# First norm, block turns and tail of a fused hash-bucket attention and gated MLP on one core

## The chip, the cores and the metric

The kernel runs on one core of a Trainium2 chip. Its time is device microseconds (us) of one execution, and the figure for a kernel is the median of its runs. The kernel before has three runs: 349.73, 350.91 and 350.99 us, median 350.91. One more execution was recorded by the profiler; it took 349.72 us.

## The reference

Four batches, eight heads, 768 tokens, head dimension 64. Every query and key gets a bucket: six sign bits of its product with a 64x6 matrix. Attention is masked to pairs with equal buckets. Its output, with the heads side by side, is the input of a normed and gated two-layer network.

```python
q_bits = (np.einsum('bhsd,dk->bhsk', q, proj) > 0)      # 6 bits; k_bits alike
mask = q_bucket[:, :, :, None] == k_bucket[:, :, None, :]
scores = np.where(mask, scale * np.matmul(q, k.transpose(0, 1, 3, 2)), -1e9)
attn = softmax(scores); x = (attn @ v) as 3072 x 512
xn = x / np.sqrt(np.mean(x * x, axis=-1, keepdims=True) + 1e-06) * rms_g
g = xn @ w_gate; silu = g * (1.0 / (1.0 + np.exp(-g)))
out = (silu * (xn @ w_val)) @ w_out                     # 512 -> 1536 -> 512
```

## The kernel before

**Units.** The work is cut into 8 units u, one for each half of the 768 queries of a batch b = u // 2. A unit has 8 heads, handled as 4 pairs hp. A slot is one third of a head of a unit: 256 keys by 384 queries. So a unit has 24 slots (NS, L545) and the main loop 192 (L750 to L755). The first two units share the order (0,0), (0,1), (1,0), (1,1), then the other heads of unit 0, then those of unit 1; from slot 48 on, unit u has slots 24u to 24u+23, which this document calls stage u-1: stage 1 is slots 48 to 71, stage 2 is 72 to 95, and so on.

**Order.** It is written out by hand. Slot t issues the scores of slot t+1 (two matmuls, L336), the exp of its own (ScalarE, L348), and then everything that the list plan[t] holds, in the order in which it was put there with at(w, s, f), which means slot 24w+s (L551). Each engine takes its instructions in that order, and waits where an input or a buffer isn't ready. The product with the values (av, L361, in two parts), the sum of the constant part of the softmax (otmp, L376), the division (rcp L381 and x L383), the squares (sq, L388) and their sums (ssp, L392) follow the scores of a head by a few slots.

**Mask.** The scores' matmul carries extra rows with the sign bits (values of +-0.5 scaled), so that pairs with equal buckets stand out by a large number in the exponent. The bits come from: a turn of q and k (64 numbers of a token onto the partitions), a matmul with the 6 columns (d_ps), signs (L209) and, for pairs that need both heads in one tile, select (L215) on VectorE, and a small DMA each to the rows of the tile QK. The turned q and k are cast to fp16 into the same tile by GpSimd (cast_part L165 for pairs of batch 0 and the first two of batch 1, cast_pool L193 for the others). The first six pairs are turned by TensorE (turn_pe, L149); all others by VectorE in blocks of 32x32 (turn_dve L180, four instructions for a pair, in slots t to t+3), from loads made in blocks (load_blocks, 8 DMAs for a pair on SyncE's queue, and one for v). hash_one (L265) makes the bits of one pair, hash_two (L282) of two. v_prep (L304) casts the values to fp16, v_sum (L309 on) adds them by thirds, and v_mean (m_ps, cvb L323) makes the constant term of the softmax for a batch. A table, spots (L638), says in which slot each pair of batches 1 to 3 is loaded and turned.

**Network.** norm(u) (L399 to L412) adds the four partial sums of squares (ss, VectorE), makes mean plus epsilon (ms, GpSimd L405) and the power -0.5 (rstd, GpSimd L409), and scales the three row blocks of x (xn, VectorE L412). turn_x (L414) turns xn on TensorE (x_ps, L419) and scales it with rms_g (xnT, VectorE). Then come 12 times gate (g_ps) and value (v_ps, both L436) with tanh on ScalarE (L444) and two products on VectorE (a L453, ht L454), and in the next unit's slots the projections (y_ps, L465, 3 x 12 matmuls) and the stores. spread (L670) deals these pieces out over the 24 slots of a stage by cost, and puts a hash in front of the first whole piece at or behind its slot. The norm of unit 0 stands at slot 36 with its turns at 38, its gates start at slot 40; the norm of unit u stands at slot 24(u+1)+4. After the last slot there is a tail: projections 0 and 1 of unit 6, norm(7), its turns with the projections of block 2 between them, the gates and the projections of unit 7.

**Buffers.** PSUM has three banks that turn_pe, hashes, m_ps, x_ps, g_ps, v_ps and y_ps share in turn (bank, L80), two for scores of two banks each (s_ps), and one for o_ps. Eight load tiles, six QK tiles.

Of the kernel before, what the change touches and what calls it, by code (L numbers as in the profile page):

```python
# [8 lines left out]
FP32 = mybir.dt.float32  # L9
FP16 = mybir.dt.float16  # L10
AF = mybir.ActivationFunctionType
ALU = mybir.AluOpType
AX = mybir.AxisListType
# [5 lines left out]
DMODEL = H * D  # L19
DFF = 1536  # L20
NF = DFF // 128
# [10 lines left out]
def kernel(  # L32
# [12 lines left out]
    nc = tc.nc  # L45
    PSUM = bass.MemoryType.PSUM

    const = ctx.enter_context(tc.tile_pool(name="const", bufs=1))
# [4 lines left out]
    xpool = ctx.enter_context(tc.tile_pool(name="xpool", bufs=2))  # L53
    npool = ctx.enter_context(tc.tile_pool(name="npool", bufs=1))
    hpool = ctx.enter_context(tc.tile_pool(name="hpool", bufs=1))
    spool = ctx.enter_context(tc.tile_pool(name="spool", bufs=2))
# [9 lines left out]
    zeros16 = const.tile([128, 512], FP16, name="zeros16")  # L66
# [2 lines left out]
    own = const.tile([128, 1], FP32, name="own")  # L69
    ebias = const.tile([128, 1], FP32, name="ebias")  # L70
    mhalf = const.tile([128, 3], FP32, name="mhalf")
    gcol = const.tile([128, 4], FP32, name="gcol")
    wg = const.tile([128, 4, DFF], FP16, name="wg")
    wv = const.tile([128, 4, DFF], FP16, name="wv")
# [5 lines left out]
    def bank(name, shape=None, dt=FP32):  # L80
        return gps.tile(shape or [128, 512], dt, name=name, tag="g")
# [242 lines left out]


    sps, psb, ot = {}, {}, {}
    x, ssp, xn, xnT = {}, {}, {}, {}

    def scores(u, i):
        b, half = divmod(u, 2)  # L330
# [38 lines left out]
    def attn_out(u, hp):  # L369
        b = u // 2  # L370
        if hp == 0:
            x[u] = xpool.tile([128, 3, DMODEL], FP32, name="x")
            ssp[u] = xpool.tile([128, 4, 3], FP32, name="ssp")
        o = ot.pop((u, hp))
        tmp = spool.tile([128, 3, 2, 66], FP32, name="otmp")
        nc.vector.tensor_add(  # L376
            tmp[:, :, :, 0:65], o[:, :, :, 0:65],
            cvb[b % 2][:, 2 * hp : 2 * hp + 2, 0:65].unsqueeze(1).to_broadcast([128, 3, 2, 65]),
        )
        r = spool.tile([128, 3, 2, 1], FP32, name="rcp")  # L380
        nc.vector.reciprocal(r, tmp[:, :, :, 64:65])  # L381
        xd = x[u][:, :, 128 * hp : 128 * hp + 128]
        nc.gpsimd.tensor_mul(  # L383
            xd.rearrange("p c (h d) -> p c h d", h=2), tmp[:, :, :, 0:64],
            r.to_broadcast([128, 3, 2, 64]),
        )
        sq = spool.tile([128, 3, 128], FP32, name="sq")
        nc.gpsimd.tensor_mul(sq, xd, xd)  # L388
        return sq

    def sumsq(u, hp, sq):
        nc.vector.tensor_reduce(  # L392
            out=ssp[u][:, hp, :], in_=sq, op=ALU.add, axis=AX.X
        )


    ht, gts = {}, {}

    def norm(u):  # L399
        ss = spool.tile([128, 3], FP32, name="ss")  # L400
        nc.vector.tensor_reduce(
            out=ss, in_=ssp[u].rearrange("p h c -> p c h"), op=ALU.add, axis=AX.X
        )
        ms = spool.tile([128, 3], FP32, name="ms")
        nc.gpsimd.tensor_scalar(  # L405
            out=ms, in0=ss, scalar1=1.0 / DMODEL, scalar2=1e-6, op0=ALU.mult, op1=ALU.add
        )
        rstd = spool.tile([128, 3], FP32, name="rstd")
        nc.gpsimd.tensor_tensor(out=rstd, in0=ms, in1=mhalf, op=ALU.pow)  # L409
        xn[u] = npool.tile([128, 3, DMODEL], FP16, name="xn")  # L410
        for c in range(3):
            nc.vector.tensor_scalar_mul(xn[u][:, c, :], x[u][:, c, :], rstd[:, c : c + 1])  # L412

    def turn_x(u, c, act=False):  # L414
        if c == 0:
            xnT[u] = npool.tile([128, 4, HALF], FP16, name="xnT", bufs=2)
        ps = bank("x_ps", [128, 4, 128], FP16)
        for kt in range(4):
            nc.tensor.transpose(ps[:, kt, :], xn[u][:, c, kt * 128 : (kt + 1) * 128], ident16)  # L419
        dst = xnT[u][:, :, c * 128 : (c + 1) * 128]  # L420
        if act:
            for kt in range(4):
                nc.scalar.mul(dst[:, kt], ps[:, kt], gcol[:, kt : kt + 1])
        else:
            nc.vector.tensor_mul(dst, ps, gcol.unsqueeze(2).to_broadcast([128, 4, 128]))
# [34 lines left out]
    def project(u, c, f0, f1):  # L460
        if f0 == 0:
            obank[u, c] = bank("y_ps")
        y = obank[u, c]
        for ft in range(f0, f1):
            nc.tensor.matmul(  # L465
                y, ht[u][:, ft, c * 128 : (c + 1) * 128], wo[:, ft, :],
                start=(ft == 0), stop=(ft == NF - 1),
            )
# [6 lines left out]
    def store(u, c):  # L475
        ysb = spool.tile([128, DMODEL], FP32, name="ysb", bufs=3)
        nc.scalar.copy(ysb, obank.pop((u, c)))  # L477
        nc.sync.dma_start(out=rows_of(u, c), in_=ysb)
# [40 lines left out]
        nc.gpsimd.memset(own[32 * t : 32 * t + 6, :], 4.0 * BIT * BIT)  # L519
    nc.vector.memset(ebias, EBIAS)  # L520
    nc.vector.memset(mhalf, -0.5)
    nc.vector.memset(ones16, 1.0)
    nc.vector.tensor_copy(ident16, ident)
    for i in range(2):
# [2 lines left out]

    wz = ops.tile([128, 512], FP32, name="z_ps", tag="o")

    def idle(n):  # L530

        for _ in range(n):
            nc.tensor.matmul(wz, zeros16[:, 0:128], zeros16, start=True, stop=True)  # L533

    idle(8)

    def load_w(dst, src, kt, n):
# [7 lines left out]
    NS = 24  # L545
# [5 lines left out]
    def at(w, s, f, *a):  # L551
        plan[NS * w + s].append(lambda: f(*a))
# [4 lines left out]
    cast_part(0, 0, "k", 1, 0, 1)  # L557
    turn_pe(0, 0, 1, "k")
    idle(3)
    sign, move, _ = hash_direct(0, 0, (0,))  # L560
    turn_pe(0, 0, 1, "q", nc.scalar.copy)
    idle(2)
    for which, e in (("k", 0), ("k", 1), ("q", 0)):
        cast_part(0, 0, which, e, 1, 1)
# [56 lines left out]
        at(0, 39 + 3 * i, load_w, wo, moe_w_out, 6 * i, 6)  # L621


    for hp, ts in ((0, (8, 22, 23, 24, 25, 24, 26, 26, 28, 38)), (1, (12, 27, 28, 29, 30, 29, 37, 31, 33, 39))):
        tl, ts = ts[0], ts[1:]
        for w in "kq":
            at(0, tl, load_natural, nc.sync, 1, hp, w)
        at(0, tl, load_v, nc.sync, 1, hp)
        at(0, ts[0], new_pair, 1, hp)
        for t, hh, w in zip(ts[0:4], (0, 1, 0, 1), "kkqq"):  # L630
            at(0, t, turn_pe, 1, hp, hh, w)
        at(0, ts[4], cast_pool, 1, hp, "k")
        at(0, ts[5], cast_pool, 1, hp, "q")
        at(0, ts[6], hash_pair, 1, hp)
        at(0, ts[7], send_pair, 1, hp)
        at(0, ts[8], v_prep, 1, hp)
        at(2, 6 + 6 * hp, v_mean, 1, hp, 2, range(6))
    spots = {  # L638
        1: ((None, None, 20, 40), (None, None, 44, 52)),
        2: ((51, 57, 66, 72), (63, 67, 81, 87)),  # L640
        3: ((96, 100, 110, 114), (105, 111, 129, 135)),
    }
    sqs = {}

    def o_step(u, hp):
        sqs[u, hp] = attn_out(u, hp)

    def s_step(u, hp):
        sumsq(u, hp, sqs.pop((u, hp)))

    at(0, 36, norm, 0)
    for c in range(3):
        at(0, 38, turn_x, 0, c)
    for n, (u, h) in enumerate(order):
# [7 lines left out]


    SCORES, AV, PROJ, FEED, TURN = 330, 290, 216, 324, 220
    hashes = {t: (700, hash_one, 1, hp) for hp, t in ((2, 49), (3, 57))}
    for b, ts in ((2, (71, 93)), (3, (117, 141))):
        for i, t in enumerate(ts):
            hashes[t] = (1430, hash_two, b, 2 * i)

# [24 lines left out]
    for u in range(7):  # L694
# [11 lines left out]
        for i in range(9):  # L706
            c, n = divmod(i, 3)
# [12 lines left out]
    for b, (loads, turns) in spots.items():  # L720
        for hp in range(4):
            if (b, hp) in ONPE:
                continue
            t = loads[hp]
            at(0, t, load_blocks, nc.sync, b, hp)
            at(0, t, load_v, nc.sync, b, hp)
            t = turns[hp]
            at(0, t, new_pair, b, hp)
            at(0, t, turn_dve, b, hp, "k", 0)
            at(0, t + 1, turn_dve, b, hp, "k", 1)  # L730
            at(0, t + 2, cast_pool, b, hp, "k")
            at(0, t + 2, turn_dve, b, hp, "q", 0)
            at(0, t + 3, turn_dve, b, hp, "q", 1)
            at(0, t + 4, cast_pool, b, hp, "q")
            at(0, t + 5, v_prep, b, hp)
            if b > 1:
                at(0, t + 5, v_sum, b, hp)
                if hp % 2:
                    at(2 * b, 1 + hp, v_mean, b, hp - 1, 4)
            else:  # L740
                at(2 * b, 6 + 6 * hp, v_mean, b, hp, 2, range(6))
# [17 lines left out]
    for c in range(2):  # L759
        project(6, c, 0, NF)  # L760
        store(6, c)
    norm(7)
    for c in range(3):
        turn_x(7, c, c == 1)
        project(6, 2, 4 * c, 4 * c + 4)
    store(6, 2)
    for ft in range(NF):
        for f in (gate, value):
# [36 lines left out]
```

## Time and profile before

| | before |
|---|---|
| median of the runs | 350.91 us (349.73 to 350.99) |
| profiled execution | 349.72 us |
| its span, first to last instruction | 347.9 us |
| mean granted TensorE clock | 0.99 |
| TensorE matmul (PE) | 331.9 us busy, 95% |
| VectorE (DVE) | 242.4 us, 70% |
| ScalarE (ACT) | 225.5 us, 65% |
| GpSimd (POOL) | 149.0 us, 43% |
| read from HBM, written | 28.32 MB, 6.29 MB |
| scores / gates and values | 94.4 / 165.6 us of PE |
| av / projections | 56.8 / 68.0 us of PE, in the group's rows (these overlap a little) |

How to read the profile. Busy times are sums over an engine's instructions; PEld is the load of TensorE's weights, which runs beside the matmuls. The page cuts the span into 40 slices of 8.70 us and gives the busy share of each in tenths (9 is 90% or more) and the granted clock in the same tenths. A row of the timeline is a run of like instructions: its start in us, its busy time, the engine, the line of the program, the operation with its output and inputs, and how often it ran; in brackets stands how long the engine had been idle before it, and what released it. A row of the windows view gives a stretch with its length and the busy time of PE, PEld, DVE, ACT and POOL with the number of instructions, the granted clock, the busy share of the DMA engines and GB/s.

### The profile page before, as it was taken

To read this page: it belongs to the slowest core of one execution; us is meant where nothing else is said; L and a number is where in the kernel's file an instruction comes from. 1 tells how busy PE (TensorE), PEld (TensorE's weight loads), DVE (VectorE), ACT (ScalarE), POOL (GpSimd) and SP (SyncE) were. 2 spreads that over 40 slices of the span, in tenths; PEclk is the share of its full clock that TensorE was granted. 3 is DMA by queue.
4 is the path that set the end of the run, shared out by engine and by line. 5 is a ranking of instruction groups with operands and counts; after the bars stand their busy time and mean duration, and the time that the engine had idled before them with its cause. 6 is when DMAs were issued, how large, how long until landed. Compare 5 with 4: busy or idle time off the path is not lost.

```text
span 347.9 us, 7717 instructions
## 1 busy us (share of the span) xinstructions
PE 331.9 (95%) x3027; PEld 200.6 (58%) x3027; DVE 242.4 (70%) x477; ACT 225.5 (65%) x327; POOL 149.0 (43%) x215
## 2 busy tenths in 40 slices
PE   8798969999999899999999999999999999998995
PEld 4465735655566355665566556655666656664554
DVE  3579957794979847996589937996566546673860
ACT  2789973566567566776677766777677867753321
POOL 4389966025433962574338632675211131122000
PEclk9999996999999999999999999999999999999999
DMA  7799947900848428001899420001100010001002
GB/s 260 279 194 293 213 92 138 179 1 25 168 92 150 88 43 204 0 3 21 174 203 166 96 77 32 2 1 51 62 0 2 2 60 32 0 3 60 33 0 92
DMA packets 78453, 31.21 MB, mean 90 GB/s; under 512 B 64736, under 2 KB 74448, under 8 KB 78416
## 3 DMA queue, kind: packets, MB, share of 16 engines
q1 hardware_dynamic: 75312, 25.73, 30.4%
q0 software_dynamic: 2656, 4.72, 7.6%
q8 instruction: 24, 0.39, 0.5%
q10 hardware_dynamic: 448, 0.27, 0.2%
q14 instruction: 13, 0.11, 0.1%
HBM read 28.32 MB, written 6.29 MB: 99 GB/s over the span
## 4 chain that ended last, share of the span: by engine, by line
PE 78%; DVE 11%; POOL 4%; issue 3%; ACT 2%; DMA 1%; POOLq 0%; DVEq 0%
PE g_ps L436 16%; PE v_ps L436 16%; PE s_ps L336 15%; PE y_ps L465 12%; PE o_ps L361 9%; PE d_ps L201 2%; PE t_ps L149 2%; PE d_ps L226 2%; PE x_ps L419 2%; ACT psb L348 1%; DVE ssp L392 1%; PE z_ps L533 1%; DVE xn L412 1%; POOL x L383 1%; POOL sq L388 1%
## 5 line engine op out<-in xcount | busy, mean ns | idle before, releaser
L348 ACT ACTIVATE psb<-s_ps,ebias 128x768 f16<-128x768 f32 x192 | 167.9, 900 | 33.7 <-PE s_ps L336 32.8
L336 PE MATMUL s_ps<-QK 76*128 76x384 f16 (+1 forms) x384 | 94.4, 327 | 4.1 <-ACT psb L348 1.5
L436 PE MATMUL g_ps<-xnT,wg 128*128 128x384 f16 x384 | 83.2, 327 | 0.1
L436 PE MATMUL v_ps<-xnT,wv 128*128 128x384 f16 x384 | 82.4, 325 | 0.8 <-DVE a L453 0.8
L444 ACT ACTIVATE t<-g_ps 128x384 f32<-128x384 f32 x96 | 47.1, 491 | 55.6 <-PE g_ps L436 55.5
L383 POOL TENSOR_TENSOR x<-otmp,rcp 128x384 f32<-128x384 f32 x32 | 26.6, 830 | 109.5 <-DVE rcp L381 109.1
L465 PE MATMUL y_ps<-wo,ht 128*128 128x512 f16 x276 | 68.0, 378 | 0.0
L453 DVE SCALAR_TENSOR_TENSOR a<-t,g_ps 128x384 f32<-128x384 f32 x96 | 52.5, 546 | 20.7 <-ACT t L444 18.7
L361 PEld LDWEIGHTS <-psb 128*128 128x128 f16 x1152 | 52.3, 98 | 18.9 <-issue 3.1
L454 DVE SCALAR_TENSOR_TENSOR ht<-a,v_ps 128x384 f16<-128x384 f32 x96 | 53.2, 554 | 10.9 <-PE v_ps L436 1.3
L361 PE MATMUL o_ps<-vl,psb 128*128 128x65 f16 x1152 | 56.8, 194 | 1.0 <-DVE otmp L376 0.9
L336 PEld LDWEIGHTS <-QK 76*128 76x128 f16 (+1 forms) x384 | 35.6, 98 | 34.1 <-issue 8.0
L436 PEld LDWEIGHTS <-wv 128*128 128x128 f16 x384 | 35.7, 97 | 23.2 <-issue 1.5
L436 PEld LDWEIGHTS <-wg 128*128 128x128 f16 x384 | 34.2, 97 | 20.4 <-issue 1.2
L465 PEld LDWEIGHTS <-ht 128*128 128x128 f16 x276 | 24.6, 97 | 22.6
L376 DVE TENSOR_TENSOR otmp<-o_ps,cvb 128x390 f32<-128x390 f32 x32 | 17.9, 559 | 15.9 <-PE o_ps L361 15.9
L388 POOL TENSOR_TENSOR sq<-x 128x384 f32<-128x384 f32 x32 | 26.5, 827 | 2.5
L392 DVE TENSOR_REDUCE ssp<-sq 128x3 f32<-128x384 f32 x32 | 17.1, 535 | 13.4 <-POOL sq L388 13.3
L477 ACT COPY ysb<-y_ps 128x512 f32<-128x512 f32 x23 | 13.5, 586 | 18.9 <-PE y_ps L465 18.9
L193 POOL CAST QK<-kT 64x768 f16<-64x768 f32 x20 | 16.4, 821 | 17.9 <-DVE kT L180 8.7
L193 POOL CAST QK<-qT 64x768 f16<-64x768 f32 x20 | 16.5, 823 | 16.6 <-DVE qT L180 12.5
L209 DVE TENSOR_SCALAR bits<-d_ps 128x384 f16<-128x384 f32 (+1 forms) x24 | 12.8, 553 | 10.2 <-PE d_ps L226 7.8
(73 smaller groups left out, 272.1 us busy)
## 6 DMA issues: line engine op xcount, KB each, us to landing
vn<-in_v_dram SPq DMA_DIRECT2D x16, 384.0 KB
out_dram<-ysb SPq DMA_DIRECT2D x23, 256.0 KB
qL<-in_q_dram SPq DMA_DIRECT2D x40, 96.0 KB
kL<-in_k_dram SPq DMA_DIRECT2D x40, 96.0 KB
kn<-in_k_dram SPq DMA_DIRECT2D x5, 384.0 KB
qn<-in_q_dram SPq DMA_DIRECT2D x5, 384.0 KB
wg<-in_moe_w_gate_dram POOLq DMA_DIRECT2D x2, 768.0 KB, 8.7
wv<-in_moe_w_val_dram POOLq DMA_DIRECT2D x2, 768.0 KB, 9.1
```

Of the source, the lines that this page charges most:

```text
L193: nc.gpsimd.tensor_copy(QK[b, 2 * hp + hh, "h"][0:64, o : o + S], src[64 * hh : 64 * hh + 64, :])
L336: nc.tensor.matmul(ps[:, j, 0:HALF], QK[b, h, "h"][0:rows, S + jt * 128 : S + (jt + 1) * 128], QK[b, h, "h"][0:rows, half * HALF : (half + ...
L348: nc.scalar.activation(psb[u, h][:, 2 * ch : 2 * ch + 2, :], sps.pop((u, i))[:, :, 0:HALF], AF.Exp, bias=ebias, scale=ESCALE,)
L361: nc.tensor.matmul(o[:, c, hh, 0:65], psb[u, h][:, jt, c * 128 : (c + 1) * 128], vls[b % 2][:, h, 2 * (jt % 3) + jt // 3 if b in PARITY el ...
L383: nc.gpsimd.tensor_mul(xd.rearrange("p c (h d) -> p c h d", h=2), tmp[:, :, :, 0:64], r.to_broadcast([128, 3, 2, 64]),)
L388: nc.gpsimd.tensor_mul(sq, xd, xd)
L392: nc.vector.tensor_reduce(out=ssp[u][:, hp, :], in_=sq, op=ALU.add, axis=AX.X)
L436: nc.tensor.matmul(ps, w[:, kt, fs], xnT[u][:, kt, :], start=(kt == 0), stop=(kt == 3))
L444: nc.scalar.activation(t, fbank[u, ft, "g_ps"], AF.Tanh, scale=0.5)
L453: nc.vector.scalar_tensor_tensor(out=a, in0=t, scalar=1.0, in1=g, op0=ALU.add, op1=ALU.mult)
L454: nc.vector.scalar_tensor_tensor(out=ht[u][:, ft, :], in0=a, scalar=0.5, in1=vv, op0=ALU.mult, op1=ALU.mult)
L465: nc.tensor.matmul(y, ht[u][:, ft, c * 128 : (c + 1) * 128], wo[:, ft, :], start=(ft == 0), stop=(ft == NF - 1),)
```

## The change

1. **Sums of squares.** The tile of the partial sums, made anew for each unit, becomes one of two constant tiles (unit parity) with a fifth column that holds 512e-6 from the start. The sum over the five is then 512 times (mean plus epsilon), so ms is left out: rstd is the power -0.5 of the sum itself, and gcol (rms_g) is scaled once by the root of 512, on GpSimd in slot 24.
2. **First norm.** The casts of q of pair (1,1) go from slot 37 to 41, its v_prep from 39 to 43 and that of pair (1,0) from 38 to 42, the hash of pair (1,1) from 31 to 32. At slots 37 and 38 two matmuls of zeros each (512 columns, into one of the three shared banks) are put in.
3. **Block turns and hashes.** The pairs of batches 1 to 3 are loaded and turned in other slots (the table spots). One pair a stage has its turns at the stage's first slots (48, 72, 96 and 120: pairs (1,2), (2,1), (3,0), (3,2)), where the projections of the unit before stand; for these four the casts, v_prep and v_sum are put five slots later than for the others. The hashes move with them.
4. **Tail.** Four projections of block 2 go ahead of the turns of unit 7's x, and three, two and three follow the three turns (before: four after each).

```diff
+    ssp = [const.tile([128, 5, 3], FP32, name=f"ssp{i}") for i in range(2)]
...
-            ssp[u] = xpool.tile([128, 4, 3], FP32, name="ssp")
...
-            out=ssp[u][:, hp, :], in_=sq, op=ALU.add, axis=AX.X
+            out=ssp[u % 2][:, hp, :], in_=sq, op=ALU.add, axis=AX.X
...
-            out=ss, in_=ssp[u].rearrange("p h c -> p c h"), op=ALU.add, axis=AX.X
-        )
-        ms = spool.tile([128, 3], FP32, name="ms")
-        nc.gpsimd.tensor_scalar(
-            out=ms, in0=ss, scalar1=1.0 / DMODEL, scalar2=1e-6, op0=ALU.mult, op1=ALU.add
+            out=ss, in_=ssp[u % 2].rearrange("p h c -> p c h"), op=ALU.add, axis=AX.X
         )
...
-        nc.gpsimd.tensor_tensor(out=rstd, in0=ms, in1=mhalf, op=ALU.pow)
+        nc.gpsimd.tensor_tensor(out=rstd, in0=ss, in1=mhalf, op=ALU.pow)
...
+    for i in range(2):
+        nc.gpsimd.memset(ssp[i][:, 4, :], DMODEL * 1e-6)
...
-    def idle(n):
-
+    def idle(n, new=None):
+
+        ps = new("z_ps") if new else wz
         for _ in range(n):
-            nc.tensor.matmul(wz, zeros16[:, 0:128], zeros16, start=True, stop=True)
+            nc.tensor.matmul(ps, zeros16[:, 0:128], zeros16, start=True, stop=True)
...
-    for hp, ts in ((0, (8, 22, 23, 24, 25, 24, 26, 26, 28, 38)), (1, (12, 27, 28, 29, 30, 29, 37, 31, 33, 39))):
+    for hp, ts in ((0, (8, 22, 23, 24, 25, 24, 26, 26, 28, 42)), (1, (12, 27, 28, 29, 30, 29, 41, 32, 33, 43))):
...
-        1: ((None, None, 20, 40), (None, None, 44, 52)),
-        2: ((51, 57, 66, 72), (63, 67, 81, 87)),
-        3: ((96, 100, 110, 114), (105, 111, 129, 135)),
+        1: ((None, None, 20, 45), (None, None, 48, 56)),
+        2: ((51, 59, 65, 76), (61, 72, 81, 87)),
+        3: ((84, 92, 100, 108), (96, 105, 120, 129)),
...
+    at(0, 24, nc.gpsimd.tensor_scalar_mul, gcol, gcol, float(DMODEL) ** 0.5)
     at(0, 36, norm, 0)
+    at(0, 37, idle, 2, bank)
+    at(0, 38, idle, 2, bank)
...
-    hashes = {t: (700, hash_one, 1, hp) for hp, t in ((2, 49), (3, 57))}
-    for b, ts in ((2, (71, 93)), (3, (117, 141))):
+    hashes = {t: (700, hash_one, 1, hp) for hp, t in ((2, 52), (3, 60))}
+    for b, ts in ((2, (80, 93)), (3, (111, 135))):
...
+            late = 5 if t % NS == 0 else 0
...
-            at(0, t + 2, cast_pool, b, hp, "k")
+            at(0, t + 2 + late, cast_pool, b, hp, "k")
...
-            at(0, t + 4, cast_pool, b, hp, "q")
-            at(0, t + 5, v_prep, b, hp)
+            at(0, t + 4 + late, cast_pool, b, hp, "q")
+            at(0, t + 5 + late, v_prep, b, hp)
...
-                at(0, t + 5, v_sum, b, hp)
+                at(0, t + 5 + late, v_sum, b, hp)
...
-    for c in range(3):
+    project(6, 2, 0, 4)
+    for c, f0, f1 in ((0, 4, 7), (1, 7, 9), (2, 9, NF)):
         turn_x(7, c, c == 1)
-        project(6, 2, 4 * c, 4 * c + 4)
+        project(6, 2, f0, f1)
```

## The prediction

> **What bounds the kernel now.** First the page: busy times, then the slices.
>
> ```profile
> PE 331.9 (95%) x3027; PEld 200.6 (58%) x3027; DVE 242.4 (70%) x477; ACT 225.5 (65%) x327; POOL 149.0 (43%) x215
> ...
> PE   8798969999999899999999999999999999998995
> ...
> PEclk9999996999999999999999999999999999999999
> ```
>
> PE is the bound: only 16.0 us of the 347.9 us span are idle. One slice has a clock of 0.6. So a gain is either PE idle time or that clock. Then the windows of TensorE around the slice (columns: PE, PEld, DVE, ACT, POOL busy, clock, DMA):
>
> ```profile
> 10.49:13.90 3.41, 2.18 (x15) 0.67 (x16) 1.58 (x5) 2.22 (x3) 0.95 (x2) 1.00 1.02 349
> ...
> 48.04:51.45 3.41, 2.00 (x24) 0.99 (x20) 0.99 (x3) 3.26 (x5) 2.37 (x5) 0.95 0.07 19
> 51.45:54.86 3.41, 1.86 (x17) 1.34 (x18) 3.41 (x5) 0.27 (x1) 2.29 (x3) 0.50 0.59 93
> 54.86:58.27 3.41, 3.41 (x28) 2.00 (x26) 1.75 (x4) 0.91 (x2) 1.47 (x2) 0.55 0.92 141
> ```
>
> The clock halves at 51.45 and comes back at 58.27, 6.83 us later. After a stretch of 3.41 us with PE busy 2.00 us it fell; after one with 2.18 us (10.49) it did not. The stretch is the first norm, in the timeline:
>
> ```profile
> 49.72 0.17 DVE L401 TENSOR_REDUCE ss<-ssp 128x3 f32<-128x12 f32 x1
> ...
> 49.99 0.19 POOL L405 TENSOR_SCALAR ms<-ss 128x3 f32<-128x3 f32 x1 [0.88 <-DVE ss L401]
> ...
> 50.26 0.89 POOL L409 TENSOR_TENSOR rstd<-ms,mhalf 128x3 f32<-128x3 f32 x1
> ...
> 51.12 1.78 POOL L165 CAST QK<-qT 64x768 f16<-64x768 f32 x2
> 51.18 2.97 DVE L412 TENSOR_SCALAR xn<-x,rstd 128x512 f16<-128x512 f32 x3 [1.29 <-POOL rstd L409]
> ...
> 52.28 0.61 PE L419 MATMUL x_ps<-ident,xn 128*128 128x128 f16 x4 [1.60 <-DVE xn L412]
> ...
> 52.97 0.90 POOL L304 CAST vl<-vn 128x768 f16<-128x768 f32 x1
> ...
> 56.93 1.30 PE L436 MATMUL g_ps<-xnT,wg 128*128 128x384 f16 x4
> ```
>
> Beside the casts the three xn take 2.97 us; in every later norm, where POOL is idle, they take 1.28:
>
> ```profile
> 86.69 1.28 DVE L412 TENSOR_SCALAR xn<-x,rstd 128x512 f16<-128x512 f32 x3 [1.28 <-POOL rstd L409]
> ```
>
> Last, the waits of stage 1 (slots 48 to 72) and of the tail:
>
> ```profile
> 89.60 0.38 PE L419 MATMUL x_ps<-ident,xn 128*128 128x128 f16 x4 [0.78 <-DVE cvb L323]
> ...
> 120.02 0.51 PE L201 MATMUL d_ps<-qT,pj 128*32 128x384 f32 x1 [0.72 <-DVE qT L180]
> ...
> 317.09 0.40 PE L419 MATMUL x_ps<-ident,xn 128*128 128x128 f16 x4 [0.93 <-DVE xn L412]
> ...
> 320.44 0.82 PE L436 MATMUL g_ps<-xnT,wg 128*128 128x384 f16 x4
> ```
>
> From slot 80 to the tail PE is idle under 0.5 us.
>
> **The change, part by part.** Sums are made against the profiled execution, 349.72 us (span 347.9). The runs are 349.73, 350.91, 350.99: it is one of the short ones, 0.34% under the median.
>
> *First norm.* Its start hardly moves: the signs go from before to behind one ssp, but still stand ahead of otmp on DVE, and their matmuls now follow av part 0 on PE; I give +0.1 us. From ss (ends 49.97) rstd follows after 0.10 without ms: 50.07 to 50.96. POOL's queue behind it now holds x of the next pair, which waits for DVE, so xn run alone: starts 0.40 apart, last one done at 52.3. Turns on PE at 51.5, 51.95, 52.35; the xnT (0.60 apart, 0.68 long) at 52.2, 52.8, 53.4; the gates at 54.13. PE needs 1.22 us between the last turn and the gates (four score matmuls 0.65, two av 0.56), done by 53.8. So **-2.8** against 56.93. The four zero matmuls (512 columns; y_ps of that size take 0.215 each) add 0.86 us to a PE that waits there; without that wait they would cost 0.86. They lift the stretch 48.04:51.45 from 2.00 to about 2.5 us busy (some of their time lies in gaps, and scores come 0.5 earlier), above 2.18: the clock should hold. At half clock PE did gate work from 56.93 to 58.27: **-0.67** more. If the clock stays half instead, the gates start at 55.2 and the gain up to 58.27 is 0.87 in all.
>
> The casts moved to slots 41 to 43 have room: POOL idles 7.88 us before 68.81, and what they feed comes at slots 54 and 58. The gcol scaling and two memsets (0.1 us each) stand where POOL waits 2.48 us.
>
> The Trainium skill (TensorE: Matmul & The Clock Gate, "What's actually happening") puts the clock down to free-running windows of 3413 ns. The 6.83 us agree with two of them. It closes the gate after an idle window; here it closed with PE 59% busy, so the measurement decides.
>
> *Stage 1.* Removed: the 0.78 at 89.60 (DVE had two kT ahead of cvb) and the broken hash at 118.45 (0.72 wait, and 2.26 us of matmuls where an unbroken hash_two takes 1.43), with 0.9 of small waits: 3.2 in all. Added: (a) The pair turned at slot 48 has kT ready before norm(1), so its casts stand directly behind rstd on POOL's queue, whatever their slot: the same place as at 51.12. The xn then take 1.04, 1.04 and 0.48, done 1.1 us later; the signs of hash_one (slot 52) wait behind them on DVE, and v_mean at slot 54 waits on PE for the signs' bank, since the other two hold y. PE comes there at 87.25 by the old clock of events, the signs end at 88.55: 1.3. (b) Slots 56 to 66 hold turns of (1,3) and (2,0) with six gate pairs and a hash: by start spacing (turn 0.72, a and ht 1.12, otmp and rcp 0.68, signs and select 1.5, ssp 0.45, cvb 0.2) 17.1 us of DVE, from 92.3 to 109.8, where PE alone would be at 109.4 with a 0.3 wait for d_ps: 0.85 of stalls. Sum: 3.2 less 2.2 is **-1.0**. With the rows' full durations in place of spacings the DVE chain is 1.8 us longer (+0.8); without (a) it is -2.3.
>
> The first scores of (1,2) (slot 59, about 96.1) need its q cast, about 95.8; those of (1,3) (slot 65, about 106) its bits: select to 102, DMA issues 0.9 apart, each landing 1.8 after its issue (packets of the issue at 97.13), so 105. Both just fit, at nothing; each us later would cost one.
>
> *Norms of stages 2, 3, 4.* Without ms 0.28 sooner, but the casts of the pair turned at slots 72, 96, 120 stand behind rstd again: first xn 0.56 later. Net 0.28, and PE already waits there (0.26 at 131.31, 0.23 at 208.01): **+0.9** for three; -0.5 if the casts miss them.
>
> The skill (SBUF — State Buffer, on the pair of ports that VectorE and GpSimd share) says that the second to issue is fully blocked. The 1.04 beside 0.48 agree. By it alone an xn that issued first would not be delayed; the first norm shows the cast first, by 0.06 us.
>
> *Slots 80 to 93.* hash_two(2,0) moves in: 2.6 us of DVE (two signs, two selects) against 1.43 of PE, where DVE was busy 21.65 of 24.30 us. DVE then has 27.3 us of work for 26.5 of PE: **+0.4** (0 to 1.2). Stages 3 and 4 lose four turns from their gates, but nothing waits there: 0.
>
> *Tail.* Four projections (0.86) fill the 0.93 wait, and xn is 0.28 sooner. Turns at 317.02, 317.9, 318.55; the last xnT ends at 319.65, gates at 319.7 against 320.44: **-0.75**. What is late next is that xnT, 0.15 behind PE.
>
> Sum: -2.8 - 0.67 - 1.0 + 0.9 + 0.4 - 0.75 = -3.9, so **345.8 us**, 1.5% under the median. I add nothing for the spread of the runs, whose cause no trace here shows.
>
> **Rivals.**
> 1. *The gate stays shut.* Zeros may not count as work, or the windows lie otherwise. For it: 2.5 us is an estimate above an edge known only between 2.00 and 2.18. Against: zeros at the head (1.18 to 4.77) precede full clock. The first norm then gives 0.87 in place of 3.47: 348.4.
> 2. *The casts miss xn*, POOL being late or xn first. Then stage 1 gives -2.3, the three norms -0.5: 343.1. Against: the queue's order, and the row at 51.12.
> 3. *A new closing of the gate (slower).* At slot 54 PE waits 1.3 us in a stretch where 1.23 to 1.41 idle closes the clock. One closing is 6.83 us at half clock on a full PE: 3.4 us, 349.2. If slots 60 to 66 close it again (late bits and DVE's queue), two closings and 0.5 to 1 us of longer waits make 353.1 to 353.6. It decides from one more us of wait in each place. Against: over 2.18 us busy kept the clock at 10.49, and window 112.89 with 0.76 of wait did too.
>
> **Numbers.** Differences within 0.5% (349.2 to 352.7 against 350.91) can hardly be told from none. Forecast 0.56; rival 1 0.14; rival 2 0.12; rival 3 once 0.11 (within), twice 0.07 (slower). Faster 0.82, same 0.11, slower 0.07. Range 343.1 (rival 2) to 349.0, which takes in rival 1 and half a us of longer waits.
>
> **What would show it.** First norm: xn 1.28 in all, gates about 2.8 sooner after ss, clock 1.00 throughout. Stage 1: xn over 2.4 with POOL casts beside; m_ps waits 1.3 for signs; no wait at the hash. Stages 2 to 4: x_ps waits about 0.5 each. Tail: x_ps without wait, g_ps 0.75 sooner after the last av. Wrong if the clock falls anywhere, or if scores wait for casts or bits.

## The result and the profile after

The changed kernel takes 348.25 us (median of 12 runs, 347.03 to 349.32); the kernel before, over 12 runs, 349.81. The ratio is 0.9949 (95% interval 0.993 to 0.9968): half a per cent faster, where 1.5% was forecast. The profiled execution took 348.43 us (span 346.7), 1.3 us less than that of before; 3.9 less was forecast. (The 3.9 are 1.1% of the profiled execution; the rest of the 1.5% is that the forecast was set against a median of three runs, 350.91, which lies 1.1 above the one of twelve.) So the direction holds, and two thirds of the gain are missing.

The page of the changed kernel:

```profile
PE 330.3 (95%) x3031; PEld 199.5 (58%) x3031; DVE 246.5 (71%) x477; ACT 225.9 (65%) x327; POOL 147.4 (43%) x210
...
PE   8798988998989999999999999999999999999996
...
PEclk9999999999999999999999999999999999999999
```

The slice with a clock of 0.6 is gone. But PE has 16.4 us without work (346.7 less 330.3), 0.4 more than before: what the first norm no longer idles, other places do. To find them, the starts of ScalarE's exp of each slot are compared in the two traces, both counted from slot 1 (the difference of two such differences is what a stretch gained or lost):

| stretch | forecast | measured |
|---|---|---|
| slots 1 to 48: first norm and clock | -3.47 | -2.89 |
| slots 48 to 96: stages 1 and 2 | -1.0 + 0.3 + 0.4 = -0.3 | +1.07 |
| slots 96 to 144: stages 3 and 4 | +0.6 | +1.76 |
| slots 144 to 191 | 0 | +0.01 |
| tail, to the issue of the last store | -0.75 | -0.85 |
| start of slot 1; end of the last store | 0 | +0.08; -0.38 |

Stages 1 to 4 were forecast at +0.3 together and cost 2.8. Of the 2.89 gained ahead of them, 0.23 lie in slots 44 to 48 and come with the new turns (experiment 2, which leaves the first norm as it was, has the same 0.23 there), so the first norm gained 2.66.

**First norm**, timeline of the changed kernel:

```profile
50.05 0.89 POOL L406 TENSOR_TENSOR rstd<-ss,mhalf 128x3 f32<-128x3 f32 x1 [0.88 <-DVE ss L402]
...
50.97 1.28 DVE L409 TENSOR_SCALAR xn<-x,rstd 128x512 f16<-128x512 f32 x3 [1.00 <-POOL rstd L406]
51.52 1.19 PE L416 MATMUL x_ps<-ident,xn 128*128 128x128 f16 x12 [0.33 <-DVE xn L409]
...
53.96 0.56 DVE L376 TENSOR_TENSOR otmp<-o_ps,cvb 128x390 f32<-128x390 f32 x1
...
54.57 0.43 PE L362 MATMUL o_ps<-vl,psb 128*128 128x65 f16 x9 [0.94 <-DVE otmp L376]
...
54.84 0.81 PE L433 MATMUL g_ps<-xnT,wg 128*128 128x384 f16 x4
```

No cast stands beside xn any more, which takes 1.28. The gates start at 54.84, not at the forecast 54.13: PE waits 0.94 for otmp, which stands on VectorE behind the three xnT, and its av is ahead of the gates. The windows of TensorE around it (columns as before):

```profile
48.03:51.44 3.41, 2.39 (x23) 1.09 (x19) 1.20 (x4) 3.07 (x4) 1.95 (x3) 1.00 0.08 21
51.45:54.86 3.41, 2.40 (x35) 1.64 (x36) 3.26 (x8) 1.21 (x2) 0.04 (x1) 1.00 0.57 91
```

**Norms of stages 1 and 3**, timeline, first of slot 52 and then of slot 100:

```profile
82.73 1.78 POOL L194 CAST QK<-kT 64x768 f16<-64x768 f32 x2
82.80 2.39 DVE L409 TENSOR_SCALAR xn<-x,rstd 128x512 f16<-128x512 f32 x3 [0.99 <-POOL rstd L406]
...
85.11 0.55 DVE L210 TENSOR_SCALAR bits<-d_ps 128x384 f16<-128x384 f32 x1
85.71 0.45 PE L321 MATMUL m_ps<-vl,ones 128*128 128x130 f16 x5 [1.14 <-DVE bits L210]
...
166.94 1.78 POOL L194 CAST QK<-kT 64x768 f16<-64x768 f32 x2
167.01 2.38 DVE L409 TENSOR_SCALAR xn<-x,rstd 128x512 f16<-128x512 f32 x3 [0.97 <-POOL rstd L406]
...
168.10 0.40 PE L416 MATMUL x_ps<-ident,xn 128*128 128x128 f16 x4 [0.29 <-DVE xn L409]
...
169.79 0.38 PE L416 MATMUL x_ps<-ident,xn 128*128 128x128 f16 x4
170.39 0.38 PE L416 MATMUL x_ps<-ident,xn 128*128 128x128 f16 x4 [0.22 <-DVE xnT L422]
```

The casts of the pair turned at slots 48, 72, 96 and 120 start with xn, and xn takes 2.4 where it took 1.3. The signs (bits) queue behind it, and m_ps waits for them; in stage 3 the three turns on PE come one by one and wait. **Slots 80 to 85**:

```profile
133.88 1.72 POOL L194 CAST QK<-qT 64x768 f16<-64x768 f32 x2
...
134.11 1.70 DVE L217 TENSOR_SCALAR bits<-bits,sel 128x768 f16<-128x768 f16 x2
...
139.57 0.48 PE L433 MATMUL v_ps<-xnT,wv 128*128 128x384 f16 x2 [0.73 <-DVE a L450]
```

The two selects of the hash moved to slot 80 take 1.70 beside a cast, and 5 us later PE waits 0.73 for a. **Tail**: no x_ps waits, and the gates start at 319.58, 0.86 sooner.

```profile
316.88 0.39 PE L416 MATMUL x_ps<-ident,xn 128*128 128x128 f16 x4
...
319.58 0.82 PE L433 MATMUL g_ps<-xnT,wg 128*128 128x384 f16 x4
```

### The profile page after: what moved, and what is told of

Read it like the earlier page. It is cut to its first block, busy times and chain, and to the rows that moved or that the text cites. A ratio compares the mean times of both kernels' runs of the same rounds, so it can differ in the third digit from the quotient of the medians.

```text
span 346.7 us, 7724 instructions
## 1 busy us (share of the span) xinstructions
PE 330.3 (95%) x3031; PEld 199.5 (58%) x3031; DVE 246.5 (71%) x477; ACT 225.9 (65%) x327; POOL 147.4 (43%) x210
## 3 DMA queue, kind: packets, MB, share of 16 engines
q1 hardware_dynamic: 75312, 25.73, 30.8%
## 4 chain that ended last, share of the span: by engine, by line
PE 73%; DVE 14%; POOL 4%; issue 3%; DMA 3%; ACT 2%; SPq 0%; DVEq 0%; POOLq 0%
PE v_ps L433 16%; PE g_ps L433 15%; PE s_ps L337 13%; PE y_ps L462 12%; PE o_ps L362 8%; DVE xn L409 3%; PE t_ps L150 2%; PE d_ps L227 2%; DMA qL<-in_q_dram 2%; DVE otmp L376 1%; ACT psb L349 1%; PE z_ps L533 1%; POOL rstd L406 1%; DVE xnT L422 1%; DVE kT L181 1%
## 5 line engine op out<-in xcount | busy, mean ns | idle before, releaser
L383 POOL TENSOR_TENSOR x<-otmp,rcp 128x384 f32<-128x384 f32 x32 | 26.5, 829 | 139.8 <-DVE rcp L381 139.3
L392 DVE TENSOR_REDUCE ssp<-sq 128x3 f32<-128x384 f32 x32 | 17.1, 535 | 7.5 <-POOL sq L388 7.4
L409 DVE TENSOR_SCALAR xn<-x,rstd 128x512 f16<-128x512 f32 x24 | 14.7, 665 | 7.8 <-POOL rstd L406 7.8
L422 DVE TENSOR_TENSOR xnT<-x_ps,gcol 128x512 f16<-128x512 f16 x23 | 14.9, 685 | 5.1 <-PE x_ps L416 5.1
L194 POOL CAST QK<-qT 64x768 f16<-64x768 f32 x20 | 16.4, 822 | 4.8 <-DVE qT L181 4.2
```

Source lines behind the costliest of these rows:

```text
L383: nc.gpsimd.tensor_mul(xd.rearrange("p c (h d) -> p c h d", h=2), tmp[:, :, :, 0:64], r.to_broadcast([128, 3, 2, 64]),)
```

## The experiments

"Slots 48-96" and "96-144" are the change of these stretches against the kernel before, from each run's trace. They repeat within 0.03 us where the code of a stretch is the same; the medians move by some tenths with the clock of the first norm.

| | kernel | median | ratio (interval) | slots 48-96 | 96-144 |
|---|---|---|---|---|---|
| | changed | 348.25 | 0.9949 (0.9930-0.9968) | +1.07 | +1.76 |
| 1 | changed, old turns | 343.66 | 0.9838 (0.9814-0.9861) | -0.60 | -0.65 |
| 2 | before, new turns | 352.93 | 1.0107 (1.0086-1.0128) | +1.71 | +2.33 |
| 3 | changed, late casts behind x | 346.13 | 0.9911 (0.9887-0.9936) | +0.84 | -0.17 |
| 4 | before, new first norm | 344.96 | 0.9872 (0.9851-0.9894) | -0.59 | -0.64 |
| 5 | changed, no zeros | 349.19 | 0.9995 (0.9979-1.0011) | +1.09 | +1.78 |
| 6 | changed, one first xnT on ScalarE | 348.25 | 0.9974 (0.9955-0.9993) | +1.10 | +1.76 |
| 7 | 1 with the hash at 80 | 342.21 | 0.9801 (0.9779-0.9823) | -1.69 | -0.65 |
| 8 | before, fifth column | 347.96 | 0.9954 (0.9938-0.9970) | -0.58 | -0.65 |
| 9 | 7, new row of batch 1 | 344.17 | 0.9843 (0.9809-0.9876) | -0.42 | -0.64 |
| 10 | 7, new row of batch 3 | 344.83 | 0.9858 (0.9829-0.9888) | -1.76 | +1.76 |
| 11 | 7, av of slot 40 later, v of (2,1) at 81 | 342.54 | 0.9792 (0.9763-0.9821) | -1.19 | -0.65 |
| 12 | 11, v of (2,1) at 83 | 342.87 | 0.9801 (0.9774-0.9828) | -1.15 | -0.65 |
| 13 | 11, v of (2,1) at 87 | 341.95 | 0.9796 (0.9781-0.9811) | -2.07 | -0.64 |
| 14 | 7, new row of batch 2 | 343.95 | 0.9853 (0.9831-0.9875) | -0.68 | -0.65 |

### Which part loses: 1, 2, 4 and 8

Experiment 1 puts the old table, the old hash slots and `late = 0` back into the changed kernel:

```diff
-        1: ((None, None, 20, 45), (None, None, 48, 56)),
-        2: ((51, 59, 65, 76), (61, 72, 81, 87)),
-        3: ((84, 92, 100, 108), (96, 105, 120, 129)),
+        1: ((None, None, 20, 40), (None, None, 44, 52)),
+        2: ((51, 57, 66, 72), (63, 67, 81, 87)),
+        3: ((96, 100, 110, 114), (105, 111, 129, 135)),
...
-            late = 5 if t % NS == 0 else 0
+            late = 0
```

> The changed kernel with the old table of loads, turns and hashes and without the late casts (first norm and tail stay changed). Theory T (the turns lose: between the starts of slots 48 and 96 the changed kernel lost 1.08 us on the one before, and 1.75 more up to slot 144): the loss comes back, so 348.25 - 2.8 = 345.4, ratio to before about 0.987; slots 96 to 144 take 77.0 us in place of 78.7. Rival R (the turns as predicted, -1.0 + 0.9 + 0.4 = +0.3, and the time went elsewhere, as to buffers or to DMAs that come earlier): 348.0 to 348.5, ratio 0.995.

343.66: more than theory T came back (the rest is told under experiment 8). Experiment 2 makes the same edit the other way round in the kernel before:

> The kernel before with nothing but the new table of loads, turns and hashes and the late casts; the first norm, ms and the tail stay as before. Theory T: the loss of slots 48 to 144 alone, +2.8, and 0.28 for each norm that still has ms where the first xn waits: 349.8 + 2.8 to 3.4 = 352.6 to 353.2, ratio about 1.009. Rival R: +0.3 to +1, so 350 to 350.8, ratio 1.001 to 1.003.

352.93, theory T. From slot 48 to 144 the turns cost 4.04 us here (1.71 + 2.33) and 4.08 in the changed kernel against experiment 1 (1.07 + 1.76 + 0.60 + 0.65): the same in both settings. The medians say 3.3 (against 349.63 for the kernel before in the same session) and 4.6, since they also hold the start of the program and the clock. Experiment 4 is experiment 1 with the old tail:

> The kernel before with the new first norm alone (sums with the fifth column, no ms, casts and hash moved, zero matmuls); turns and tail as before. Theory T (the slots before 48 gained 2.88 us in the changed kernel): 349.8 - 2.9 = 346.9, ratio 0.992; with 0.28 sooner xn in the other norms up to 0.4 us less, and nothing given back behind. Rival G (what the first norm gains is given back later, since the stages behind wait for loads or VectorE that don't come sooner): under 1.5 us less, 348.3 or more.

344.96, 1.5 us less than theory T at its lowest, which gave the fifth column up to 0.4 behind the first norm. Experiment 8 makes that edit alone (no ms, `in0=ss` in rstd, the fifth column, gcol scaled):

> The kernel before with nothing but the fifth column: no ms, rstd on the sum itself, gcol scaled. Theory: 0.28 us in each norm whose x_ps PE waits for (slots 39, 55, 78, 126 and the tail), in sum 1.2 to 1.6 us, and the clock still falls in the first norm: 349.7 - 1.4 = 348.3, ratio 0.996. Rival (xn waits for the casts or for VectorE anyway, and the 0.28 is worth nothing outside the tail): 349.4, ratio 0.999.

Theory: 347.96. Slots 48 to 144 get 1.23 us shorter by the column alone, since with the old turns PE's waits at the turns of x (x_ps) in slots 55, 78 and 126 (0.78, 0.26, 0.23) shrink to 0.48, 0 and 0 and the stops with them. In the changed kernel this gain was there and covered by the larger loss. In the pair 4 and 1 the tail is worth the wait of x_ps, 0.65 us in experiment 4 and none in 1.

### Casts beside xn: 3, 9, 10 and 14

Experiment 3, in the changed kernel, for the four pairs:

```diff
-            at(0, t + 2 + late, cast_pool, b, hp, "k")
+            at(0, t + 2 + (7 if late else 0), cast_pool, b, hp, "k")
...
-            at(0, t + 4 + late, cast_pool, b, hp, "q")
+            at(0, t + 4 + (6 if late else 0), cast_pool, b, hp, "q")
```

> The changed kernel with the casts of the four pairs turned at slots 48, 72, 96 and 120 put behind x of the stage's first pair on the GpSimd queue (k nine slots after the turn's first, q ten). Theory C (the casts beside xn are what the stages 1 to 4 lose): xn 1.28 in every norm, the 1.1 us wait of m_ps and the waits of 0.2 to 0.5 us of x_ps gone, 2.3 to 3.0 us less than the changed kernel: 345.3 to 346.0, ratio to before about 0.988. Rival D (VectorE's own load decides: four turns more ahead of the norm, or the casts now slow the products instead): under 1 us less, 347.3 to 348.3, ratio 0.993 to 0.996.

Its timeline at the norm of slot 52:

```profile
84.49 1.28 DVE L409 TENSOR_SCALAR xn<-x,rstd 128x512 f16<-128x512 f32 x3 [0.99 <-POOL rstd L406]
...
86.29 0.51 PE L321 MATMUL m_ps<-vl,ones 128*128 128x130 f16 x6
...
95.13 0.48 PE L337 MATMUL s_ps<-QK 76*128 76x384 f16 x2 [1.21 <-POOL QK L194]
```

xn takes 1.28 in every norm, and behind the first norm m_ps and x_ps no longer wait. The median lies just above theory C's range, since the later q cast brings a wait of its own, 1.21 us of the scores of (1,2). Slots 48 to 144 are 2.2 us shorter than in the changed kernel. Slots 96 to 144, with no new wait, come back by 1.93 of the 2.41 that lie between the changed kernel and experiment 1.

The rows one by one, each put into experiment 7 (below), in which only the old turns run:

> The kernel of experiment 7 (old turns, hash at 80; 342.21) with only the new loads, turns, late casts and hashes of batch 1 (pairs (1,2) at slot 48 and (1,3) at 56). Theory C (stage 1 pays for the casts beside xn): xn 2.4 in the norm of slot 52, m_ps waits 1.1 us for the signs, d_ps 0.2; with what PE loses at each stop 1.5 to 2.0 us: 343.7 to 344.2. Rival (stage 1 was a gain, as the prediction had it, since the waits at the old 89.60 go): 342.2 or less.

> The kernel of experiment 7 with only the new loads, turns, late casts and hashes of batch 3 (turns at 96, 105, 120, 129). Theory C (a collision of casts and xn costs the whole 1.1 us that the three xn take longer, and PE's stops, not the 0.3 of the prediction): xn 2.4 in the norms of slots 100 and 124, three waits of x_ps in each, slots 96 to 144 longer by 2.0 to 2.4: 344.2 to 344.6. Rival (the prediction's 0.56 for the first xn alone): 1.1 longer, 343.3.

> The kernel of experiment 7 with only the new loads, turns and late casts of batch 2 (turns at 61, 72, 81, 87; the hash is at 80 in both). By difference this row should cost what experiments 9 and 10 leave of the whole (5.2 between slots 48 and 144, less 1.3 and 2.4): 1.5 us, 343.7. Theory C: the norm of slot 76 with xn 2.4 and x_ps waits of 0.5 and 0.1, selects of slot 80 of 1.7 beside the casts and a wait of v_ps of 0.7. Rival (the rows are not independent, and stage 2 loses only when stage 1 has filled VectorE's queue): under 0.7, 342.2 to 342.9.

Slots 48 to 144 grow by 1.28, 2.34 and 1.01 us. In each case theory C's rows are there (m_ps 1.15; x_ps 0.30, 0.10, 0.22 and 0.48, 0.14; x_ps 0.51 and 0.14, v_ps 0.74; the first of these x_ps waits 0.41 in experiment 7 already, behind a v_sum that experiment 11 moves, so it tells little by itself), though by the traces 9 and 14 cost less than the 1.5 to 2.0 and 1.5 expected. The three make 4.6 of the 5.2 between experiment 7 and the changed kernel; the rest was not tried by itself.

### Casts beside the selects: 7, 11, 12 and 13

Experiment 7 is experiment 1 with the first hash of batch 2 where the changed kernel has it:

```diff
-    for b, ts in ((2, (71, 93)), (3, (117, 141))):
+    for b, ts in ((2, (80, 93)), (3, (117, 141))):
```

> The kernel with the old turns of the first experiment (343.66), and its first hash of batch 2 moved from slot 71 to 80, where the changed kernel has it. Theory V (the signs and selects of that hash overload VectorE in slots 80 to 93): waits of v_ps for a of 0.7 and 0.2 us at about 138 and 152 as in the changed kernel, some 1.2 us with what PE loses at each stop; the broken hash at slot 71 (0.72 of wait and 0.74 of longer matmuls) goes: 343.4 to 343.7. Rival W (those waits came from the late casts and turns, not from the hash): no wait in slots 80 to 93, 342.2 to 342.5.

Rival W: the hash itself was a gain. Its timeline:

```profile
131.59 0.88 DVE L217 TENSOR_SCALAR bits<-bits,sel 128x768 f16<-128x768 f16 x2
...
136.27 0.48 PE L433 MATMUL v_ps<-xnT,wv 128*128 128x384 f16 x2 [0.18 <-DVE a L450]
```

The selects run alone here, in half the time, and the wait is 0.18, with one of 0.16 behind it. Experiment 11 makes two moves, and one of them puts v_prep and v_sum beside the selects:

```diff
+            late = 9 if (b, hp) == (2, 1) else late
             at(0, t + 5 + late, v_prep, b, hp)
...
-            at(0, 3 * n + 4 + part, av, u, h, part)
+            at(0, 41 if n == 12 else 3 * n + 4 + part, av, u, h, part)
```

> The kernel of experiment 7 with the av of slot 40 one slot later, behind the first gates, and v_prep and v_sum of pair (2,1) at slot 81 in place of 72, behind x. Theory Q (PE waits 0.94 for otmp ahead of gates whose xnT is done 0.5 sooner; and the v_sum ahead of x in GpSimd's queue makes the norm of slot 76 late by 0.4): both go, 0.47 + 0.41 and what PE loses at a stop, 342.2 - 1.0 = 341.2. Rival (the wait moves behind the gates, and the v casts slow the xnT): 342.0 to 342.3.

```profile
130.16 1.81 DVE L217 TENSOR_SCALAR bits<-bits,sel 128x768 f16<-128x768 f16 x2
...
135.73 0.48 PE L433 MATMUL v_ps<-xnT,wv 128*128 128x384 f16 x2 [0.73 <-DVE a L450]
```

342.54, which is above both. The av moved behind the gates gained 0.48 up to slot 42 and the norm of slot 76 no longer waits; both went again at 135.73. Experiment 12 set `late = 11`:

> The kernel of experiment 11 with v_prep and v_sum of pair (2,1) two slots later still, at 83 and so behind the selects of the hash of slot 80 on GpSimd's queue. Theory P (in experiment 11 the two selects took 1.78 us beside v_prep and v_sum, 0.84 in experiment 7 without them, and that made the new wait of v_ps, 0.73 us at 135.73): the selects take 0.84 again, that wait falls to 0.2, and the kernel takes 342.4 - 0.9 = 341.5, 0.3 to 0.9 under experiment 7. Rival (VectorE is late there by the turns of slot 81, whatever GpSimd does): the wait stays and the time is 342.2 to 342.6.

342.87, and nothing in the trace had moved: GpSimd was idle, so the v casts started directly behind sq again, two slots later in the list or not. This tells nothing about theory P. Experiment 13 set `late = 15`, which puts them behind x of slot 86, an instruction that waits:

> The kernel of experiment 11 with v_prep and v_sum of pair (2,1) behind the casts of pair (2,2) and x of slot 86 on GpSimd's queue, so that its waits hold them back (two slots later alone had not moved them: they had started directly behind sq as before). Theory P (the selects of the hash of slot 80 beside v_prep and v_sum make the wait of 0.73): the two selects take 0.84 in place of 1.78, the wait is 0.2 or less and slots 84 to 96 are 0.7 to 0.9 shorter: 342.5 - 0.8 = 341.7. Rival (the turns of slot 81 make VectorE late, whatever GpSimd does): the wait of 0.73 stays, 342.3 to 342.7.

```profile
130.71 0.88 DVE L217 TENSOR_SCALAR bits<-bits,sel 128x768 f16<-128x768 f16 x2
...
135.38 0.48 PE L433 MATMUL v_ps<-xnT,wv 128*128 128x384 f16 x2 [0.18 <-DVE a L450]
```

Theory P: the wait of 0.73 is gone, and slots 48 to 96 are 0.88 us shorter than in 11. With 341.95 us this is the fastest median, 2.0% under the kernel before; its interval overlaps that of experiment 7.

### The clock and the first norm: 5 and 6

Experiment 5 takes the two lines `at(0, 37, idle, 2, bank)` and `at(0, 38, idle, 2, bank)` out of the changed kernel.

> The changed kernel without the four matmuls of zeros at slots 37 and 38. Theory Z (their work in PE's waits keeps the clock): the stretch that holds the first norm falls to about 1.4 us busy, the clock is half for at least 3.41 us in every execution (mean clock 0.990 to 0.995), and the kernel is 0.7 to 1.7 us slower than the changed one, 349.0 to 350.0, ratio to before 0.997 to 1.000. Rival (the zeros only fill a wait, and the clock goes its own way): the mean clock is 1.0 in two of three executions as with them, and the time 348.0 to 348.4.

Theory Z, nearly: 11 of 12 executions have a mean clock under 1.0 (median of these 349.26), where the changed kernel has 4 of 12 (348.9; the 8 at 1.0 have 347.9). In the trace of experiment 5 the clock is half from 53.01 to 56.42, behind a stretch with PE busy 2.17 us, not 1.4. So the zeros hold the clock in two executions of three, and in the third it falls, as in rival 1 of the prediction. No trace of those four was kept; where other kernels with the zeros have a fall in their trace (experiments 1, 3, 4, 6, 10, 13), it is one stretch of 3.41 us at the first norm, between 48 and 58 us, with none after it up to the last two us. Experiment 6 scales the middle xnT on ScalarE: `at(0, 38, turn_x, 0, c, c == 1)`.

> The changed kernel with the second xnT of the first norm scaled on ScalarE (four instructions, 1.14 us in the tail) and not on VectorE. Theory Q (what is late after the first norm's casts are gone is otmp of slot 39, queued behind three xnT on VectorE; PE waits 0.94 us for it ahead of the av of slot 40): otmp starts 0.6 sooner, the wait of o_ps at 54.57 falls to 0.2 to 0.4 us and the kernel gains 0.4 to 0.6: 347.6 to 347.9. Rival (the four instructions hold the exp of slot 40 back on ScalarE by up to 1.1 us, and PE waits for that): 348.2 to 348.8.

The rival:

```profile
52.80 1.14 ACT L420 ACTIVATE xnT<-x_ps,gcol 128x128 f16<-128x128 f16 x4 [2.61 <-PE x_ps L416]
...
54.79 0.48 PE L337 MATMUL s_ps<-QK 70*128 70x384 f16 x2 [1.26 <-ACT psb L349]
```

PE no longer waits for otmp and now waits 1.26 for an exp that stands behind those four instructions. The median is that of the changed kernel. (In this execution the clock was half from 49.02 to 52.43, ahead of these rows.)

## Why the forecast was too good, step by step

- **The step that failed: "Norms of stages 2, 3, 4 ... first xn 0.56 later. Net 0.28."** The place was right (the casts do stand directly behind rstd, whatever their slot), the price was not. Two of three xn double, so the last is 1.1 us late, not 0.56, and the turns on PE wait up to three times in a norm. The forecast has this 1.1 itself, in stage 1 ("1.04, 1.04 and 0.48, done 1.1 us later"), and priced the later norms by the first xn alone. Waits grew by 0.62 us in stage 3 and 0.41 in stage 4 and PE lost 0.42 and 0.31 more beside them: 1.04 and 0.72 where 0.3 each was forecast. Slots 96 to 144 lost 1.76, and experiment 10 shows the same 1.76 with these turns alone.
- **The stops themselves were left out.** I counted waits as PE's idle time only. Counting each PE instruction from its start to the next start, less idle, PE's rows also grew in the changed kernel: net 0.7 us in slots 48 to 96 (the 0.74 that the broken hash gave back set aside), and the 0.42 and 0.31 just told. The growth sits in the last matmul ahead of each stop: a projection matmul starts 0.215 us after the one before it, but its row is 0.38 long, and when PE has to wait behind it (at 169.31, before the turn at 169.79), the profile counts idle time only from the row's end. So a stop costs about 0.16 us more than the idle time shown. (The ends of matmuls are modelled in the profile; the sum of both parts is what was measured.)
- **"Slots 80 to 93: +0.4 (0 to 1.2)."** Measured 1.0 of waits, inside that range. The two selects were priced near what they took (2.6 less two signs of 0.55 leaves 1.5; 1.67 measured), but the 27.3 and 26.5 of the sum don't follow from the numbers beside them (21.65 + 2.6 is 24.25, 24.30 + 1.43 is 25.73). What I did not ask is why selects take that long: the casts made late stand beside them. Alone the two take 0.84 (experiment 7). Experiments 13 and 11 show 0.88 against 1.81 us for the rows of the two, and 0.18 against 0.73 of wait.
- **First norm: 2.66 in place of 3.47.** xn and the casts came as forecast, and so did the clock in the profiled execution. "What is late next" was not asked on VectorE's queue: otmp behind the xnT, 0.94 of wait ahead of the gates. Moving that av behind the gates gave back 0.48 (experiment 11).
- **Stage 1: -1.0 was right.** The 3.2 that go are the old waits (2.44) and the broken hash (0.74 of longer matmuls); the 2.15 that come are m_ps 1.14 (forecast 1.3) and two VectorE waits of 0.23 and 0.78 (forecast 0.85, from a sum with a slip in it: 17.1 us from 92.3 end at 109.4, not 109.8). The gain is the hash's: its move to slot 80 makes slots 48 to 96 shorter by 1.09 (experiment 7 against 1), while the new row of batch 1 by itself costs 1.28 (9 against 7).
- **Tail: right**, -0.85 for -0.75.
- **The clock: the edge between 2.00 and 2.18 us does not stand.** The rows of the prediction have a clock of 0.95 in 48.04:51.45 and of 0.55 in 54.86:58.27, so the clock fell at 51.09 and came back at 57.92, 0.36 us sooner than I read (the gate work at half clock was worth 0.5, not 0.67). The stretches of 3.41 us that fit these times, in the kernel before:

```profile
10.13:13.55 3.41, 1.97 (x13) 0.49 (x13) 1.61 (x4) 2.34 (x3) 1.31 (x2) 1.00 1.02 349
...
47.68:51.09 3.41, 2.36 (x26) 1.25 (x24) 0.72 (x2) 3.26 (x5) 2.37 (x4) 1.00 0.08 21
51.09:54.50 3.41, 1.51 (x12) 0.98 (x12) 3.32 (x4) 0.63 (x1) 2.65 (x4) 0.50 0.52 83
```

The clock fell after 2.36 us of busy PE (69% of the stretch, not 59%) and held after 1.97. In experiment 1 it fell after 2.01 (44.94:48.35), in experiment 11 it held after 2.10 (45.20:48.61). PE's busy time alone gives no edge in these traces, and what decides stays open. That the zeros help is shown by experiment 5; the reason given for it (2.5 us, above 2.18) is not, and that the profiled execution was one that held is luck. Rival 1 was given 0.14 for every execution alike and a price of 2.6 us; the clock fell in a third of them, at about 1 us. A forecast of a median needs the share, which one trace can't tell.
- **Rival 2** (the casts miss xn) is what experiment 3 makes: 2.1 us under the changed kernel, where the rival gave 2.7, with a new wait of 1.21 in it. In the changed kernel itself nothing of the kind happened: the first cast started 0.06 to 0.08 us ahead of xn in all four norms.
- **Rival 3** (a new fall of the clock at slot 54) shows in no trace: in the changed kernel the stretch with the wait of m_ps, 84.84 to 88.25, has 2.54 us of busy PE and a clock of 1.00.

So the change is three gains (column 1.6 us by experiment 8, first norm, tail) and one loss of 4 (the new turns and hashes, experiments 1 and 2), which the forecast took for nearly nothing. Without the new turns the same kernel is 1.6% faster than before.

## What to carry to other kernels

An operation's slot in a hand-written order says when it is issued, not when it runs: on an engine that idles it runs with whatever releases the instruction ahead of it, and so meets the same neighbour each time. To move it, put it behind an instruction that waits. And when two engines disturb each other, price the whole group of instructions behind them and every stop that the bounding engine makes for it, not the first one's delay.

## What the runs showed of the hardware

Not every VectorE operation suffers beside GpSimd. Beside its casts xn goes from 0.48 to 1.03 us, and a select of the hash of slot 80 from 0.42 (experiment 7) to 0.80 and 0.87 (changed kernel), while a takes 0.55 with GpSimd busy or idle, ht 0.55, otmp 0.56, and the block turns 0.88 beside GpSimd and 0.87 alone. The Trainium skill (SBUF — State Buffer, "SBUF: two separate sides") says that on VectorE only operations in a two-port mode, or with two SBUF inputs, contend with GpSimd; these rows agree for xn and select, and a, ht and otmp read PSUM. By the same page of the Trainium skill whoever comes second waits for the whole instruction of the first. Here xn, issued 0.06 us behind the cast, ends 0.28 after it, less than the 0.48 that it takes alone, so some of it ran beside the cast: the measurement decides. A full wait would make xn about 1.23 long (an estimate, 0.75 of cast left and 0.48); the prediction's 1.04 agrees with that rule in direction only.

The start of slot 1 lay between 9.8 us (experiment 1) and 11.4 us (experiment 2) in the profiled executions, a spread as large as the whole change; so traces are compared here from slot 1 on, and kernels by medians.
